# Reordering the head of a fused linear-attention + gated-unit kernel: first halves of two v projections ahead of their second halves, two tiles averaged ahead of either's centring

## Chip, cores, metric

One core of a Trainium2 chip. The metric is device time in microseconds (us) for one execution. "Fast" is the undisturbed state of a run; all comparisons use fast runs. The span is the time from the first to the last instruction of a profiled execution; the granted clock is the share of full speed that TensorE was allowed.

## The reference, cut to what matters

```python
def reference(A_x, A_wqkv, A_w_phi, A_wo, B_x, B_w_gate, B_w_up, B_w_down):
    xn = _layernorm(A_x, axis=-1)                  # 2048 tokens x 512
    # _A_ref: qkv = xn @ wqkv; softmax feature maps of q and k (32 heads of 16); linear attention; @ wo
    # _B_ref: ((xn @ w_gate) * (xn @ w_up)) @ w_down, inner width 1792
    return A_x + _A_ref(xn, ...) + _B_ref(xn, ...)
```

## The kernel before

The 2048 tokens are 16 tiles of 128. Only the first microseconds matter here. Tiles 0 to 3 are centred as soon as x lands (ACT and DVE each average one half of tiles 0 to 2), turned by TensorE (PE), copied by ACT or DVE out of PSUM (the memory that PE writes to), and multiplied by the v weights. Their scaling by the standard deviation is done later.

A v projection of one tile is four 128x512 matmuls into one PSUM bank. The first half of them (h = 0) reads the first half of the v weights and the first half of the tile's turned columns; the second half (h = 1) reads the others. The two halves of the weights are two DMAs.

```python
    load_x(0, 1)                 # on SP
    load_x(1, 1, ACT)
    load_x(2, 2)
    load_v(SP, 1)                # second half of the v weights, 256 KB
    load_gu(SP, 0, (1,))         # first up weights
    act(sbf("lnv", 0, 1), eps_f, ["eps"], ["pace"])
    load_v(ACT, 0)               # first half of the v weights, 256 KB
    load_gu(ACT, 0, (0,))        # first gate weights
    # ... cut: further loads on SP

    def ln_mean_split(t):        # ACT: sum of columns 256.. ; DVE: sum of columns ..256
        act(xn_tile(t)[:, 256:], x_tile(t)[:, 256:], [("x", t)], [("mu", t)], scale=1.0 / 512.0,
            accum=mu[:, t:t + 1])
        dve(lambda e: e.tensor_scalar(out=xn_tile(t)[:, :256], ..., accum_out=mua[:, t:t + 1]),
            [("x", t)], [("mua", t)], 256)

    def ln_center_split(t):      # two DVE instructions of 256 columns
        for h in range(2):
            dve(lambda e, hs=hs: e.tensor_scalar(..., op0=ALU.subtract, op1=ALU.subtract),
                [("x", t), ("mua", t), ("mu", t)], [("xn", t, h)], 256, 0.27)

    def v_matmul(t, b, hs=(0, 1)):
        for h in hs:
            mm(bank(b), [(xnT(q, t * 128, 128), wv_v[:, q, :]) for q in (2 * h, 2 * h + 1)],
               ([("xnT", t, h)] if t < 2 else [("xnT", t)]) + [("wv", h)], b, start=h == 0, stop=h == 1)

    warm(7)
    warm(1, 512, [("x", 0)])
    sc.pin = True                # from here on the order written is the order run, on every engine
    ln_mean_split(0)
    ln_center_split(0)
    ln_mean_split(1)
    ln_center_split(1)
    ln_mean_split(2)
    x_transpose(0, 2, 0, 2)      # tile 0, bank 2, half 0; copied out by ACT
    x_transpose(0, 3, 1, 2)
    warm(1, 256)                 # a matmul on constants, meant to keep PE's clock up
    x_transpose(1, 4, 0, 2, DVE)
    x_transpose(1, 5, 1, 2, DVE)
    warm(1, 256)
    ln_center_whole(2)
    ln_mean(3)
    ln_center(3)
    v_matmul(0, 0)
    v_matmul(1, 1, (0,))
    x_transpose(2, 6)
    v_matmul(1, 1, (1,))
    # ... cut: two up/gate units in halves, v of tiles 2 and 3, then the long main part
```

The softmax here doesn't subtract the row's maximum and nothing guards it: scores larger than these inputs give would overflow.

## Time and profile before

| | before |
|---|---|
| time | 221.97 us, median of 3 (221.96 to 222.13) |
| profiled span | 219.8 us, granted clock 1.0 |
| PE busy | 215.8 us |

From the profile page, part 1 (busy us, share of the span, instructions by engine) and part 4 (the chain of waits, share of the span by engine):

```profile
PE 215.8 (98%) x1276; PEld 105.3 (48%) x1276; DVE 143.0 (65%) x251; ACT 87.6 (40%) x168; POOL 53.7 (24%) x119
...
PE 96%; DMA 2%; SPq 0%; issue 0%; DVE 0%
```

PE and PEld are TensorE's matmuls and weight loads, DVE, ACT and POOL the other engines, SPq the queue that issues DMAs. PE is the bound almost everywhere, so time can only be saved where PE idles. The timeline of PE in the head shows start, length, line and shapes, and in brackets PE's idle time and what ended it (L441 are the transposes, L670 the warm-ups, L224 the projections):

```profile
4.60 0.54 PE L441 MATMUL ps<-arena 128*128 128x128 bf16 x4 [0.20 <-DVE arena L392]
4.98 0.27 PE L670 MATMUL ps<-const-bfloat16-1.0 128*128 128x256 bf16 x1
5.58 0.54 PE L441 MATMUL ps<-arena 128*128 128x128 bf16 x4 [0.32 <-DVE arena L392]
5.96 0.27 PE L670 MATMUL ps<-const-bfloat16-1.0 128*128 128x256 bf16 x1
6.06 0.59 PE L224 MATMUL ps<-arena 128*128 128x512 bf16 x2
7.00 1.02 PE L224 MATMUL ps<-arena 128*128 128x512 bf16 x4 [0.34 <-DMA arena<-in_A_wqkv_dram]
```

There are three gaps. The two matmuls at 6.06 are v of tile 0, first half; the four from 7.00 are its second half and v of tile 1, first half. Which gap costs time is told by the chain that ended last (start, length, what), its first pieces:

```profile
1.70 5.16 DMA arena<-in_A_wqkv_dram
6.86 0.14 issue
7.00 1.02 PE ps L224 x4
8.02 0.22 PE ps L441 x4
```

The chain goes from PE at 7.00 to the DMA of the second v weights, issued at 1.70 and landed at 6.86. It touches neither DVE nor the transposes: shortening the gaps at 4.60 and 5.58 would only lengthen the one at 7.00.

### The profile page before, as it was taken

What the parts mean: (1) busy time and instruction counts of PE and PEld (TensorE: products, weight loads), DVE (VectorE), ACT (ScalarE), POOL (GpSimd) and SP (SyncE); (2) the same over time, 40 slices, a digit from 0 to 9 for tenths busy, and PEclk for the clock granted to TensorE, in tenths of its full rate; (3) what the DMA queues carried; (4) which work ended last, traced back from release to release, by engine and by line L of the source; (5) the groups of instructions that cost most, each with busy time, mean ns of one, the idle gap of its engine ahead of it and who ended that gap; (6) DMA issues with size and microseconds to landing.
All of it is one profiled execution on the core that took longest, in us unless ns stands there. A gap on an engine that the chain in (4) does not pass through costs nothing.

```text
span 219.8 us, 3329 instructions
## 1 busy us (share of the span) xinstructions
PE 215.8 (98%) x1276; PEld 105.3 (48%) x1276; DVE 143.0 (65%) x251; ACT 87.6 (40%) x168; POOL 53.7 (24%) x119
## 2 busy tenths in 40 slices
PE   7999999999999999999999999999999999999995
PEld 2574444444444444544444444544454444454453
DVE  3846899989176654675486565797867777445341
ACT  5558965468753435333445525531122211000000
POOL 3031274323122202220241422224332222200000
PEclk9999999999999999999999999999999999999999
DMA  5998582039910000000002220333764555342221
GB/s 188 277 313 277 146 194 49 0 63 352 185 25 0 0 3 0 0 0 3 0 0 49 48 48 2 73 73 77 162 144 101 116 108 115 84 103 73 64 59 48
DMA packets 47249, 19.91 MB, mean 91 GB/s; under 512 B 37504, under 2 KB 46720, under 8 KB 47232
## 3 DMA queue, kind: packets, MB, share of 16 engines
q1 hardware_dynamic: 46288, 19.03, 36.6%
q10 hardware_dynamic: 944, 0.66, 1.0%
q8 instruction: 10, 0.16, 0.3%
q14 instruction: 7, 0.06, 0.1%
HBM read 8.67 MB, written 2.10 MB: 49 GB/s over the span
## 4 chain that ended last, share of the span: by engine, by line
PE 96%; DMA 2%; SPq 0%; issue 0%; DVE 0%
PE ps L224 91%; DMA arena<-in_A_wqkv_dram 2%; PE ps L569 2%; PE ps L522 2%; PE ps L336 1%; SPq L249 0%; PE ps L441 0%; DVE arena L651 0%
## 5 line engine op out<-in xcount | busy, mean ns | idle before, releaser
L224 PE MATMUL ps<-arena 128*128 128x512 bf16 (+3 forms) x962 | 207.2, 371 | 0.3 <-DMA arena<-in_A_wqkv_dram 0.3
L224 PEld LDWEIGHTS ps<-arena 128*128 128x128 bf16 x962 | 90.9, 98 | 98.4 <-ACT arena L205 0.8
L205 ACT ACTIVATE arena<-ps 128x512 bf16<-128x512 f32 (+3 forms) x116 | 64.4, 594 | 87.6 <-PE ps L224 74.5
L472 DVE TENSOR_REDUCE arena<-arena 128x64 f32<-128x1024 bf16 x32 | 38.5, 1213 | 21.6 <-ACT arena L205 21.6
L627 DVE TENSOR_TENSOR arena<-ps,arena 128x512 bf16<-128x512 f32 x56 | 38.3, 686 | 20.9 <-PE ps L224 17.1
L482 POOL TENSOR_TENSOR arena<-arena 128x512 bf16<-128x512 bf16 x32 | 33.8, 1056 | 1.2
L480 POOL TENSOR_TENSOR arena<-arena 128x32 f32<-128x32 f32 x32 | 8.5, 266 | 96.4 <-DVE arena L476 51.0
L651 DVE TENSOR_TENSOR arena<-ps,arena 128x512 bf16<-128x512 f32 (+2 forms) x13 | 8.5, 651 | 21.5 <-PE ps L224 21.5
L205 ACT ACTIVATE arena<-arena 128x512 bf16<-128x512 bf16 (+4 forms) x31 | 14.6, 495 | 4.1 <-DMA arena<-in_A_x_dram 1.9
L205 ACT ACTIVATE arena<-ps,arena 128x512 bf16<-128x512 f32 x16 | 10.0, 686 | 5.7 <-PE ps L224 5.7
L590 DVE TENSOR_TENSOR arena<-ps,arena 128x512 bf16<-128x512 f32 x16 | 11.1, 692 | 0.6
L363 DVE BATCH_NORM_STATS2 arena<-arena 128x6 f32<-128x512 bf16 x16 | 10.4, 667 | 0.0
L510 DVE TENSOR_TENSOR arena<-ps,arena 128x512 bf16<-128x512 f32 x14 | 9.0, 641 | 0.0
L476 DVE RECIPROCAL arena<-arena 128x64 f32<-128x64 f32 x16 | 8.5, 534 | 0.0
L522 PEld LDWEIGHTS ps<-arena 128*128 128x128 bf16 x128 | 6.2, 97 | 3.8
L569 PEld LDWEIGHTS ps<-arena 128*128 128x128 bf16 x128 | 6.2, 97 | 3.8
L569 PE MATMUL ps<-arena 128*128 128x68 bf16 x128 | 6.7, 194 | 0.0
L522 PE MATMUL ps<-arena 128*128 128x68 bf16 x128 | 6.7, 194 | 0.0
L589 DVE RECIPROCAL arena<-arena 128x32 f32<-128x32 f32 x16 | 5.6, 353 | 0.6
L421 POOL TENSOR_SCALAR arena<-arena 128x1 f32<-128x1 f32 x12 | 2.9, 265 | 12.2 <-ACT arena L205 12.2
L478 DVE RECIPROCAL arena<-arena 128x32 f32<-128x32 f32 x16 | 5.4, 345 | 0.2
L580 POOL TENSOR_SCALAR arena<-arena 128x32 f32<-128x32 f32 x4 | 1.2, 291 | 16.3 <-DVE arena L472 16.3
(35 smaller groups left out, 43.8 us busy)
## 6 DMA issues: line engine op xcount, KB each, us to landing
out_dram<-arena SPq DMA_DIRECT2D x15, 128.0 KB, 1.7
arena<-in_B_w_down_dram SPq DMA_DIRECT2D x1, 1792.0 KB, 8.0
arena<-in_A_x_dram SPq DMA_DIRECT2D x3, 512.0 KB, 3.8
arena<-arena SPq DMA_TRANSPOSE x44, 3.1
arena<-in_B_w_gate_dram SPq DMA_DIRECT2D x1, 640.0 KB, 8.7
arena<-in_B_w_up_dram SPq DMA_DIRECT2D x1, 640.0 KB, 9.7
arena<-in_B_w_gate_dram SPq DMA_DIRECT2D x1, 512.0 KB, 5.0
arena<-in_B_w_up_dram SPq DMA_DIRECT2D x1, 512.0 KB, 6.0
```

Source lines behind the costliest of these rows:

```text
L205: return sc.step(ACT, lambda e: e.activation(out=out_ap, in_=in_ap, func=func, scale=scale, **kw), reads, writes, 130.0 + 0.833 * n)
L224: ins = e.matmul(out_ap, lhsT=l, rhs=r, start=start and i == 0, stop=stop and i == npair - 1, **kw)
L363: dve(lambda e: e.bn_stats(stats_v[:, t, 0:6], x_tile(t)), [("x", t)], [("st", t)], 512)
L472: dve(lambda e: e.tensor_reduce(out=sm, in_=e_v, axis=AX.X, op=ALU.add), [(name, s, 0), (name, s, 1)], [("sums", sr)], 1024)
L476: dve(lambda e: e.reciprocal(out=rs, in_=sm), [("sums", sr)], [("rs", s)], 64, 6.5)
L480: pool(lambda e: e.tensor_tensor(out=rat, in0=sm[:, :, 0], in1=rs[:, :, 1], op=ALU.mult), [("sums", sr), ("rs", s)], [("rat", s)], 32)
L482: pool(lambda e: e.tensor_tensor(out=e_v[:, :, 1, :], in0=e_v[:, :, 1, :], in1=rat[:, :, None].to_broadcast([128, H, 16]), op=ALU.mult), [ ...
L510: dve(lambda e: e.tensor_tensor(out=vs_tile(t)[:, :, 0:16], in0=src.rearrange("p (h f) -> p h f", h=H), in1=rp.unsqueeze(2).to_broadcast([ ...
L522: ins = e.matmul(bank(c // 4, (c % 4) * CW, CW), lhsT=ek[:, c * 128:(c + 1) * 128], rhs=vs[:, c * CW:(c + 1) * CW], start=(t == 0 and c % ...
L569: ins = e.matmul(bank(b0 + c // 4, (c % 4) * CW, CW), lhsT=ph[:, c, :], rhs=kvz_v[:, c, :], start=True, stop=True)
L590: dve(lambda e: e.tensor_tensor(out=o_tile(t).rearrange("p (b h f) -> p b h f", b=2, f=16), in0=nd[:, :, :, 0:16], in1=w_v[:, r].unsqueeze ...
L627: dve(lambda e: e.tensor_tensor(out=hT_v[:, ft, sg * 512:(sg + 1) * 512], in0=bank(bu), in1=g, op=ALU.mult), [("ps", bu), ("g", s)], [("hT ...
```

## The change

The intent is to have v of tile 1, first half, run in the gap before the second weights land, and to have its data there in time. Both tiles are averaged before either is centred, the average of tile 2 (which waits for a later piece of x) goes behind the copies out of PSUM, and the two warm-ups are halved.

```diff
     ln_mean_split(0)
+    ln_mean_split(1)
     ln_center_split(0)
-    ln_mean_split(1)
     ln_center_split(1)
-    ln_mean_split(2)
     x_transpose(0, 2, 0, 2)
     x_transpose(0, 3, 1, 2)
-    warm(1, 256)
+    warm(1, 128)
     x_transpose(1, 4, 0, 2, DVE)
     x_transpose(1, 5, 1, 2, DVE)
-    warm(1, 256)
+    warm(1, 128)
+    ln_mean_split(2)
     ln_center_whole(2)
     ln_mean(3)
     ln_center(3)
-    v_matmul(0, 0)
+    v_matmul(0, 0, (0,))
     v_matmul(1, 1, (0,))
+    v_matmul(0, 0, (1,))
     x_transpose(2, 6)
     v_matmul(1, 1, (1,))
```

## The prediction

> **What bounds the kernel now.** TensorE: busy 215.8 of the 219.8 us span (page, part 1); the chain of waits is 96% PE. From 7.00 us to the last matmul, PE's start-to-start spacings (timeline) never exceed one matmul, so only the head can win. PE idles there 0.2 us before the transposes of tile 0 (start 4.60), 0.32 before those of tile 1 (5.58), and 0.34 before the second half of tile 0's v projection (7.00, released by the weights' DMA). The chain runs back from 7.00 to that DMA (issued 1.70, all parts landed 6.86), not to DVE or ACT: the two earlier gaps are off it.
>
> **What the change does.** No work goes except two warm-up matmuls cut from 256 to 128 columns.
> - Now: v0 first half (two 128x512 matmuls, from 6.06), wait, at 7.00 v0 second half, v1 first half, transposes of tile 2, v1 second half. Matmuls start 0.2155 us apart, as the Trainium skill's "TensorE: Matmul & The Clock Gate", "Back-to-back issue gap", gives (N/2.4 + 2.5 ns: 216 ns at 512).
> - After: v1's first half needs only the first half of the weights (landed 5.63) and tile 1's first transposed half, so it runs in the gap. After the landing PE has two matmuls less: 2 x 0.2155 = 0.43 us.
>
> **Does the head deliver?** My estimate from the trace's durations and pitches: averaging both tiles first puts tile 0's centring 0.1 later (4.20 to 4.30), its transposes at 4.70; tile 1's centring comes 0.35 earlier (5.17 to 4.82), transposes at 5.22. Tile 2's average no longer stands before the evictions on ACT (it waited for x until 5.08), so they start near 5.1 instead of 5.49. v0 first half then waits for its weights: about 5.77. Tile 1's copies on DVE end near 5.9 and 6.15, so v1's first half runs about 6.20 to 6.63. v0's second half stays at about 7.00, idle before it 0.34 to 0.4. Tile 2 is centred by 6.9, before its transposes at 7.43.
>
> **Is it kept?** What follows moves up by 0.43 and must find its data: gate weights landed 7.72 (needed 8.08), up weights 8.52 (needed 9.6), evictions of tiles 2 and 3 follow PE, the key fold has over 2 us of slack. After that PE is the bound, so the gain should survive.
>
> **Predicted time: 221.55 us** (221.97 - 0.43), 80% range 221.3 to 221.95. Chances: faster by over 2% 0.01, within 2% 0.98, slower by over 2% 0.01.
>
> **What would show each step right or wrong.**
> - v0 second half still starts at about 7.0, released by the weights' DMA.
> - v1 first half lies wholly before it; tile 2's transposes start at about 7.43 (before: 7.86), the first up projection at 8.08 (before: 8.51).
> - PE's span is shorter by 0.43 from there on, with no new idle.
> - Tile 0's transposes start about 0.1 later, tile 1's about 0.35 earlier.
>
> **What would make it wrong.**
> - The landing moves from run to run; with an early one in unprofiled runs the old order lost less: gain 0.3 or below.
> - Tile 2's centring or the gate weights come late: gain 0.1 to 0.3.
> - The clock, granted full from 4.72 us on: less warm-up work could lose it. The same page, "The HAM clock gate", gives windows of about 3.4 us and half rate; one would cost up to 1.7 us (estimate). Unlikely: idle stays under 0.4 us at a time.
> - Unpinned DVE/ACT work is reordered by the kernel's own scheduler; PE's slack should hide that.

## The result, and the profile after

| | before | after |
|---|---|---|
| time, median of 6 | 221.91 us (221.41 to 222.13) | 221.51 us (220.91 to 221.63) |
| ratio, 95% interval | | 0.998 (0.9965 to 0.9995) |
| profiled span | 219.8 us | 219.7 us |

Ratios here and below are the mean time of one kernel's fast runs over the mean of the other's of the same rounds, so they are not quite the ratios of the medians.

The medians differ by 0.40 us, the means by 0.44. The profiled spans differ by only 0.1 us, and the trace tells why. PE's timeline in the changed kernel:

```profile
4.69 0.65 PE L441 MATMUL ps<-arena 128*128 128x128 bf16 x4 [0.30 <-DVE arena L392]
5.14 0.31 PE L670 MATMUL ps<-const-bfloat16-1.0 128*128 128x128 bf16 x1
5.24 0.63 PE L441 MATMUL ps<-arena 128*128 128x128 bf16 x4
5.67 0.31 PE L670 MATMUL ps<-const-bfloat16-1.0 128*128 128x128 bf16 x1
5.79 1.33 PE L224 MATMUL ps<-arena 128*128 128x512 bf16 x4
7.31 0.59 PE L224 MATMUL ps<-arena 128*128 128x512 bf16 x2 [0.18 <-DMA arena<-in_A_wqkv_dram]
```

Four 128x512 matmuls now stand before the wait and two behind it, instead of two and four. The wait ends at 7.31 instead of 7.00, because in this execution the weights landed later. The chain:

```profile
1.71 5.46 DMA arena<-in_A_wqkv_dram
7.17 0.14 issue
7.31 0.59 PE ps L224 x2
7.90 0.22 PE ps L441 x4
```

So the profiled execution lost 0.31 us to a later landing and won the rest back. This can be freed of the luck of the landing: take the span minus the start of v0's second half (both from the instruction records, which have more digits than the page). Before: 219.85 - 7.00 = 212.85 us. After: 219.72 - 7.31 = 212.42 us, rounded from 212.415. The difference is 0.43 us, which is two matmuls at the spacing of 0.2155 us.

One caution on the page after: its trace holds 1252 matmul records where the trace before holds 1276, so its PE busy time (214.8 us) and a few small gaps in its chain come from missing records, not from idle time.

### The profile page after: what moved, and what is told of

The parts are those of the page before. It is cut to its first block, busy times and chain, and to the rows that moved or that the text cites. A ratio compares the mean times of both kernels' runs of the same rounds, so it can differ in the third digit from the quotient of the medians.

```text
span 219.7 us, 3305 instructions
## 1 busy us (share of the span) xinstructions
PE 214.8 (98%) x1252; PEld 105.6 (48%) x1276; DVE 143.2 (65%) x251; ACT 87.8 (40%) x168; POOL 53.9 (25%) x119
## 4 chain that ended last, share of the span: by engine, by line
PE 95%; DMA 2%; issue 1%; SPq 0%; DVE 0%
PE ps L224 90%; DMA arena<-in_A_wqkv_dram 2%; PE ps L569 2%; PE ps L522 2%; PE ps L336 1%; SPq L249 0%; PE ps L441 0%; DVE arena L651 0%
## 5 line engine op out<-in xcount | busy, mean ns | idle before, releaser
L224 PE MATMUL ps<-arena 128*128 128x512 bf16 (+3 forms) x938 | 205.2, 372 | 1.5 <-DMA arena<-in_A_wqkv_dram 0.2
L224 PEld LDWEIGHTS ps<-arena 128*128 128x128 bf16 x962 | 91.0, 98 | 98.4 <-ACT arena L205 0.7
```

Of the source, the lines that this page charges most:

```text
L224: ins = e.matmul(out_ap, lhsT=l, rhs=r, start=start and i == 0, stop=stop and i == npair - 1, **kw)
```

## The experiments

Twelve runs were made, in three calls of four (E1 to E4; the changed kernel again, E5, E9, E10; E9 again, E11, E12, E8). Each call has its own runs of the kernel before. The three calls ran on three different chips, so times are best compared within a call. Names: v0 and v1 are the v projections of tiles 0 and 1. Theory A is the prediction's: two matmuls pass from behind the landing to ahead of it. Theory B says the gain comes from the new averages and the earlier tile 1. Theory C says both parts are needed.

This table has all the traces but those of E3 and E4, in which the clock fell (us; "landing" is the last of the 16 parts of the second v weights).

| run | order of halves | landing | start of v0's second half | span | span minus start |
|---|---|---|---|---|---|
| before | old | 6.86 | 7.00 | 219.85 | 212.85 |
| E2 head only | old | 7.35 | 7.49 | 220.34 | 212.85 |
| E10 | old | 6.45 | 6.59 | 219.45 | 212.86 |
| E12 | old | 6.25 | 6.39 | 219.24 | 212.85 |
| after | new | 7.17 | 7.31 | 219.72 | 212.42 |
| changed kernel again | new | 7.24 | 7.38 | 219.80 | 212.42 |
| E1 order only | new | 7.41 | 7.55 | 219.95 | 212.40 |
| E9 | new | 6.31 | 6.55 | 218.97 | 212.42 |
| E9 again | new | 6.47 | 6.73 | 219.15 | 212.42 |
| E11 | new | 6.42 | 6.88 | 219.30 | 212.42 |
| E8 no warm-ups | new | 6.86 | 6.99 | 219.57 | 212.58 |
| E5 tile 2 ahead too | new | 7.12 | 7.17 | 219.56 | 212.39 |

### E1: the new order of the halves alone

Kernel before with:

```diff
-    v_matmul(0, 0)
+    v_matmul(0, 0, (0,))
     v_matmul(1, 1, (0,))
+    v_matmul(0, 0, (1,))
```

> The kernel before with the new order of the v projection's halves alone; averages, centring and warm-ups as before. Theory A (two matmuls, 0.43 us, pass from behind the landing of the second weights to ahead of it): full gain, 0.35 to 0.43 us against before; in its trace v1's first half starts near 6.5, v0's second half 0.13 after the landing. Rival B (the gain is tile 1's earlier centring and transposes): gain under 0.15 us. Rival C (both are needed, as the matmuls come too late without the new head): 0.1 to 0.3 us, and v0's second half starts later than landing + 0.14.

Measured: 221.47 us (before 221.76), ratio 0.9987, interval 0.9969 to 1.0005. The mean gain is 0.29 us, which misses theory A's 0.35 to 0.43 and lies in theory C's range; the interval reaches zero, so the time alone would not settle it. The trace does. PE's timeline of E1:

```profile
6.13 1.03 PE L224 MATMUL ps<-arena 128*128 128x512 bf16 x4
7.55 0.59 PE L224 MATMUL ps<-arena 128*128 128x512 bf16 x2 [0.39 <-DMA arena<-in_A_wqkv_dram]
```

Four matmuls ahead of the wait, and after it the 212.40 us of the changed kernel, with the old head. v1's first half was started at 6.56, as expected. Theory B fails on the trace, and at this landing (7.41) C does too: v0's second half started 0.14 us behind it. With the old head PE is through with v1's first half at 6.99 in this trace, so C could only hold for landings before about 6.86 (estimate). That the mean gain is 0.14 us short of 0.43 would follow if E1's runs had later landings than those of the kernel before; landings of unprofiled runs are not on record.

### E2: the new head alone

Changed kernel with the three `v_matmul` lines put back:

```diff
-    v_matmul(0, 0, (0,))
+    v_matmul(0, 0)
     v_matmul(1, 1, (0,))
-    v_matmul(0, 0, (1,))
```

> The changed kernel with the old order of the v halves: new averages, centring and short warm-ups alone. Theory A: no gain (within 0.15 us of before): v0's first half starts near 5.8 instead of 6.06, but its second half still 0.13 us after the landing, and PE waits there 0.25 us longer than before. Rival B: gain of 0.3 us or more.

Measured: 222.12 us, ratio 1.0025, interval 0.9996 to 1.0053. No gain, as theory A has it, though the expected 0.15 us either way was missed on the slow side. PE's timeline of E2:

```profile
5.98 0.59 PE L224 MATMUL ps<-arena 128*128 128x512 bf16 x2 [0.23 <-DMA arena<-in_A_wqkv_dram]
7.49 1.02 PE L224 MATMUL ps<-arena 128*128 128x512 bf16 x4 [0.92 <-DMA arena<-in_A_wqkv_dram]
```

The better head only waits longer (0.92 us), and what follows the wait is the 212.85 us of the old order. The expectation that v0's first half starts near 5.8 was missed (5.98), because its own weights landed at 5.84. One of the six timed runs took 223.81 us at a granted clock of 0.992; the other five average 222.05, still 0.25 us over the mean of before (221.80). Whether this rest is a chance of the landings was not settled.

### E3 and E4: the second weights later, with the new and with the old order

In the changed kernel (E3) and in the kernel before (E4):

```diff
-    load_v(SP, 1)
     load_gu(SP, 0, (1,))
+    load_v(SP, 1)
```

> The changed kernel with the second half of the v weights issued after the first up weights, so that it lands later (about 8.5 instead of 6.9 to 7.2). Theory A: the time moves with the landing, about 1.3 to 1.7 us slower than the changed kernel, and is 0.43 us under the next run of this call (same delay, old order). A theory that the landing does not bound expects no loss.

> The kernel before with the same delay of the weights. Theory A: 1.3 to 1.7 us slower than before, as v0's second half starts 0.13 us after the later landing, and 0.43 us slower than the run with the new order and the same delay. Rival B (earlier tile 1 is what counts): as slow as that one.

Measured: E3 223.66 us (222.39 to 224.98), ratio 1.0077, interval 1.0035 to 1.0118. E4 224.43 us (223.35 to 233.96), ratio 1.0116, interval 1.0081 to 1.0150. The delay costs time, as theory A has it, but the sizes cannot be read, because something else came in. Three of six E3 runs, and two of the five fast E4 runs, had a granted clock of 0.992 (E4's sixth run, 233.96 us, was slow; its execution is the one profiled). E3's three runs at full clock average 222.60 us; its three at 0.992 average 224.72. E4's three fast runs at 0.999 or 1.0 average 223.73 us (223.35 to 223.96), 1.13 us over E3's three at full clock. The sign agrees, but the distance is over twice the expected 0.43 us, and with so few runs, and no fast trace of E4, it stays unexplained.

The trace of E3 shows the clock. First PE's timeline, then busy times by stretch (PE, PEld, DVE, ACT, POOL, granted clock, DMA share, GB/s):

```profile
5.77 1.02 PE L224 MATMUL ps<-arena 128*128 128x512 bf16 x4
8.62 0.90 PE L224 MATMUL ps<-arena 128*128 128x512 bf16 x2 [1.83 <-DMA arena<-in_A_wqkv_dram]
```

```profile
5.40:8.70 3.30, 1.36 (x9) 0.52 (x8) 3.06 (x11) 1.23 (x5) 0.00 (x0) 1.00 1.07 338
8.80:12.10 3.30, 3.30 (x17) 2.07 (x16) 1.39 (x4) 0.60 (x1) 0.78 (x3) 0.50 1.25 232
12.20:15.60 3.40, 3.35 (x24) 2.35 (x24) 0.00 (x0) 2.10 (x5) 1.10 (x4) 1.00 0.90 313
```

In the first stretch PE was busy 1.36 of 3.30 us, and in the next the clock was half. Its record falls to 0.5 at 8.77 us and comes back at 12.18. The Trainium skill's "TensorE: Matmul & The Clock Gate", section "The HAM clock gate", describes such windows of 3413 ns, and the record's 3.413 us agrees to the digit. In this trace the span minus the start of v0's second half is 214.10 us, 1.68 more than in the traces at full clock: half of 3.41 us. A wait for weights can thus be followed by a cost of its own. That the long wait brings it about rests on counts: 5 of the 11 fast runs with late weights had the clock of 0.992, one of E2's six, and one of the 33 runs of the kernel before.

### The changed kernel again

> The changed kernel once more, as the yardstick of this call and for a second trace. Theory A: 0.2 to 0.6 us under before; whatever its landing is, the span minus the start of v0's second half is 212.41 us (0.01 to 0.03 either way), as in the two earlier traces with the new order, against 212.85 in the two with the old.

Measured: 221.37 us (before 221.75), ratio 0.997, interval 0.9934 to 1.0006. One of the eleven runs of before took 224.01 us at a clock of 0.992; without it, the means are 221.75 and 221.28, a gain of 0.46 us. The trace gives 212.42 us after the start of v0's second half, as expected.

### E5: the transposes of tile 2 into the gap too

```diff
-    v_matmul(0, 0, (1,))
     x_transpose(2, 6)
+    v_matmul(0, 0, (1,))
     v_matmul(1, 1, (1,))
```

> The changed kernel with the transposes of tile 2 (four of 128 columns, 0.22 us) ahead of v0's second half too. Theory A: span minus the start of v0's second half falls by another 0.22 us, to 212.19; but tile 2 is centred at about 6.99 us, so its transposes start at about 7.05 and end at 7.27: with a landing after 7.13 the gain is up to 0.22 us, with one at 6.9 it is nothing. On average 0 to 0.2 us under the changed kernel. A rival by which the number of matmuls after the landing does not matter expects none at any landing.

Measured: 221.35 us, ratio 0.9973, interval 0.9942 to 1.0005; as fast as the changed kernel of the same call (means 221.32 and 221.28). The transposes did run in the gap, earlier than expected:

```profile
6.73 0.40 PE L441 MATMUL ps<-arena 128*128 128x128 bf16 x4
7.17 1.64 PE L224 MATMUL ps<-arena 128*128 128x512 bf16 x8
```

The first line is the four transposes of tile 2. The eight matmuls of the second line (the piece names only the first one's shape) are four of v and the four half-width ones of the first gate projection; they take 1.64 us to the end of the last. In the records the first gate matmul starts 0.38 us after the last v matmul instead of 0.22, so PE stood still for 0.16 us; the gate weights had landed 0.05 us before it started (8.16 and 8.21). The 0.22 us won was mostly lost to the next transfer in line: span minus start came to 212.39, not the expected 212.19.

### E9 and E10: the first gate weights out of the way

Changed kernel (E9) and kernel before (E10) with:

```diff
-    load_gu(SP, 0, (1,))
+    load_gu(SP, 0)
     act(sbf("lnv", 0, 1), eps_f, ["eps"], ["pace"])
     load_v(ACT, 0)
-    load_gu(ACT, 0, (0,))
```

The gate weights are needed after all the v weights, but on ACT's queue they flowed at the same time. The Trainium skill's "DMA: Bandwidth & Descriptors", "Issuing engines are not separate DMA queues", says that transfers of all issuing engines run on the same 16 DMA engines and interleave; now the SP queue has them in the order of need.

> The changed kernel with the first gate weights taken from ACT's queue and issued on SP behind the second v weights, so that these need not share the DMA engines with them. If the landing bounds: it comes near 6.2 instead of 6.9 to 7.2, v0's second half starts at about 6.65, right behind v1's first half, and the first up projection at about 7.75 instead of 7.96 to 8.08: 0.3 to 0.6 us under the changed kernel. If the gate weights then land after 7.6, part of it is lost; if the transfers are bound by something other than sharing, the landing stays and so does the time.

> The kernel before with the same earlier landing of the second v weights. Theory A: with the wait gone, the order of the halves is worth nothing any more: v0's second half starts at about 6.50 behind its first half, the first up projection at about 8.0; 0.5 to 0.8 us under before, and only 0.2 to 0.3 us behind the run of the changed kernel with the same loads (that rest is the earlier start of v0's first half, 5.79 against 6.06). If the change were worth its 0.43 us whatever the landing, that distance would be 0.43 us.

Measured: E9 220.84 us, ratio 0.9954, interval 0.9922 to 0.9985. E10 221.22 us, ratio 0.9971, interval 0.9940 to 1.0003. The second v weights landed at 6.31 and 6.45 instead of 6.86 to 7.41, as the page would have it. Sharing may not be all: in E9 the gate weights, issued 0.44 us later than in the trace after, landed earlier too (7.20 and 8.25), and the bytes moved in the first 8 us hardly differ between the traces (1.76 to 1.85 MB with the old loads, 1.82 to 1.88 with the new). Why was not settled. PE's timeline of E9 has no wait any more:

```profile
5.69 1.46 PE L224 MATMUL ps<-arena 128*128 128x512 bf16 x6
6.98 0.39 PE L441 MATMUL ps<-arena 128*128 128x128 bf16 x4
7.21 1.03 PE L224 MATMUL ps<-arena 128*128 128x512 bf16 x6
```

The first six are v0's first half, v1's first half and v0's second half, back to back. Its chain of waits has moved away from those weights and, as the view has it, into the head:

```profile
0.79 2.60 DMA arena<-in_A_x_dram
...
3.41 0.57 DVE arena L385 x3
...
4.18 0.27 DVE arena L392
...
4.50 0.54 PE ps L441 x4
5.04 0.06 PE ps L670
5.09 0.46 PE ps L441 x4
5.55 0.06 PE ps L670
5.61 0.08 issue
5.69 1.46 PE ps L224 x6
```

The view puts x, the averages (L385), the centring (L392) and even the warm-ups (L670) on the chain. But the 0.08 us called "issue" before 5.69 hide a wait for the other half of the v weights. From the DMA view of E9 (KB, us from issue to landing; issued at 1.28 on ACT and 1.71 on SP):

```profile
arena<-in_A_wqkv_dram ACTq DMA_DIRECT2D x1, 256.0 KB, 4.3
arena<-in_A_wqkv_dram SPq DMA_DIRECT2D x1, 256.0 KB, 4.6
```

In the records the first half landed at 5.555 and v0's first half started at 5.690, 0.135 us later, though its columns had been copied by 5.20. This distance is 0.135 or 0.136 us in all nine traces with the new head, and 0.235 to 0.432 us in the five with the old one. So the new head is good enough to wait for the first v weights, and in E9 their landing, with six matmuls back to back behind it, is the bound. E9 is 0.40 us under the changed kernel of its call (means 220.88 and 221.28), and the fastest kernel.

For E10 the expectation was partly wrong. It said that the wait would be gone, so that the distance to E9 would be 0.2 to 0.3 us. But E10's weights landed at 6.45, still later than its first half was done, and v0's second half still started 0.135 us behind the landing. Its means are 0.39 us behind E9 (221.27 and 220.88). The wait had become shorter, not gone.

### E9 again, E11 and E12: which part counts once the weights come early

E11 is E1 with the loads of E9; E12 is E2 with the loads of E9.

> The changed kernel with the first gate weights behind the v weights, once more, as yardstick: 0.7 to 1.1 us under before. v0's second half right behind v1's first half (near 6.55), span minus its start 212.41 us.

> New order of the halves with the old averages and centring, gate weights behind. With the weights landing near 6.3 to 6.45, PE gets to v0's second half late by itself: v0's first half starts at 5.94 to 6.06 (old head), v1's first half 0.43 later, v0's second half at 6.8 to 6.9, no wait for the DMA. So 0.25 to 0.35 us slower than the yardstick: at an early landing the new head, worth nothing before, is worth that much.

> New averages and centring with the old order of the halves, gate weights behind. v0's first half near 5.7, its second half at the landing + 0.135, so 6.45 to 6.6; span minus that start 212.85. Against the yardstick 0.3 to 0.45 us slower, about like the old head and old order with the same loads (221.22 in the call before), for which the landing binds too.

| with the loads of E9 | old order of halves | new order |
|---|---|---|
| old head | E10 221.27 | E11 221.10 |
| new head | E12 221.13 | E9 again 220.86 |

These are mean times; E10 was in the call before, on another chip, in which E9 gave 220.88. Medians and ratios to the kernel before: E9 again 220.85, 0.9945 (0.9923 to 0.9968); E11 221.02, 0.9956 (0.9933 to 0.9980); E12 221.16, 0.9959 (0.9935 to 0.9983). The new order alone is now worth 0.17 us, and both parts together about 0.4. The 0.14 us between E10 and E12 is no gain of the head: in both traces v0's second half starts 0.135 us behind the landing, with 212.85 or 212.86 us to follow, and E12's weights landed 0.20 us earlier (6.25 and 6.45). The head pays only on top of the new order (E11 to E9 again), and the order pays less without the head; so at an early landing theory C holds in part. E11 is 0.24 us behind E9 (0.25 to 0.35 was expected), E12 0.27 us (0.3 to 0.45 was expected). The first lines of L224 in E11 and of the wait in E12 show the two reasons:

```profile
6.02 1.46 PE L224 MATMUL ps<-arena 128*128 128x512 bf16 x6
```

```profile
5.63 0.59 PE L224 MATMUL ps<-arena 128*128 128x512 bf16 x2
6.39 1.02 PE L224 MATMUL ps<-arena 128*128 128x512 bf16 x4 [0.17 <-DMA arena<-in_A_wqkv_dram]
```

E11 starts its six matmuls late (6.02, 0.33 us behind the first landing) and has no wait; E12 starts early (5.63, 0.135 us behind it) and then waits. In the trace of E9 again v0's second half started at 6.73, not near 6.55, as the first v weights landed at 5.73 instead of 5.555; the 212.42 us after it came as expected.

### E8: no short warm-ups

Changed kernel without both `warm(1, 128)` lines.

> The changed kernel without the two short warm-up matmuls of 128 columns. They stand in idle time of PE, so if the clock does not fall back the time is that of the changed kernel (within 0.15 us; 0.2 to 0.6 us under before), and granted clock 1.0 in all runs. If they keep the clock up, some runs show a clock of 0.992 and 1.5 to 2 us more, as the runs did in which PE waited 1 to 2 us for the weights.

Measured: 221.51 us (221.16 to 223.12), ratio 0.9984, interval 0.9953 to 1.0015. The granted clock was 0.999 or 1.0 in all six runs, so taking them out did not make the clock fall here; six runs cannot exclude a rare fall. The one run of 223.12 us had a clock of 1.0 and is not explained; so had one of 223.46 us of the kernel before.

The trace holds a second lesson. The weights landed early (6.86), v1's second half was done early, and the six matmuls from there on took

```profile
7.64 1.19 PE L224 MATMUL ps<-arena 128*128 128x512 bf16 x6
```

instead of the 1.03 us of the six at 7.21 in E9. The first gate projection waited 0.15 us, and its weights had landed at 8.18, 0.05 us before its start. This is why E8's line in the table reads 212.58.

## Why the prediction was right

The predicted time was 221.55 us, the measured one 221.51; the predicted gain was 0.43 us, the measured difference of the medians 0.40, of the means 0.44.

- **The bound in the head is the landing of the second v weights.** Right. In the traces with a wait there, v0's second half starts 0.13 to 0.14 us behind the landing, wherever that is between 6.25 and 7.41 (E5, which has the transposes in between, is the exception with 0.05).
- **Two matmuls, 0.43 us, leave the part behind the landing.** Right, and the best-shown point: span minus start is 212.85 or 212.86 us in four traces with the old order, and 212.40 to 212.42 in six with the new, with either head and either order of loads.
- **The head's gaps are off the chain.** Right for the loads as they were: the head alone (E2) gave no gain. Once the second weights land early, a slow head does cost time if the order is the new one (E11 against E9 again).
- **v0's first half waits for its weights, about 5.77.** Right: 5.79, 0.135 us behind their landing.
- **v0's second half at about 7.00.** The cause was right, the time was not: 7.31 in that execution; tile 2's transposes (7.74) and the first gate projection (8.39, in the prediction "the first up projection") were as late against 7.43 and 8.08. A single trace had been read as if the landing were fixed, and its landing was an early one: that execution took 221.57 us, 0.40 less than the median of the timed runs. By the constant rest a landing near 7.26 goes with the median (estimate). The predicted gain does not depend on it as long as v1's first half is done before the landing.
- **v1's first half from 6.20 to 6.63.** It ran from 6.53 in the trace after, because full clock was granted only at 6.42 us, not at 4.72 as in the trace before; with full clock at 5.73 (the changed kernel again) it ran from 6.21. Its delay was hidden in the wait, with some luck: PE was through with it at 6.96, and with the landing of the trace before (6.86, start at 7.00) only 0.04 us would have been left.
- **Tile 0's transposes 0.1 us later, tile 1's 0.35 earlier.** 0.09 later and 0.33 earlier.
- **The data that follow are there in time.** Right in the two traces of the changed kernel, but with less room than the prediction gave. It took the gate weights to land at 7.72, 0.36 us before they were needed. In the trace after they landed at 8.25 and the gate projection started at 8.39; in E5 and E8 they cost 0.15 to 0.16 us.
- **The clock as a risk.** It did not strike the changed kernel in 12 runs. That it is real is shown by E3.

What stays open: the distance between E3 and E4, why the landing of one transfer moves by up to 0.55 us between executions whose loads are the same, and whether the shorter wait makes the fall of the clock rarer than in the kernel before (one of the 33 runs of before had a clock of 0.992, none of 12 of the changed kernel: too few to tell).

## What to carry to other kernels

When the chain of waits runs to a landing, the gain of a reordering is the work that passes from behind that landing to ahead of it, and time saved upstream of the landing only lengthens the wait. Compare two traces from the moment of the landing on, not from the start: a constant remainder shows an effect of 0.4 us that timings with a scatter of the same size hardly do. Then look at the order of the transfers themselves: putting a later-needed load behind the needed one gave 0.40 us more, and made the new head matter, which alone had gained nothing, on top of the new order. And check a chain of waits against the landings themselves: the one of E9 runs through warm-ups, while the start of v0's first half keeps the same distance from the landing of its weights in nine traces.

## What the Trainium skill lacked or had wrong

- "TensorE: Matmul & The Clock Gate", "Why this matters for your kernels", asks for no PE idle gaps of over about 3 us. In E3 (one trace) a single gap of 1.83 us in a window in which PE was busy 1.36 of 3.30 us was followed by 3.41 us at half clock, and the three runs with a clock of 0.992 took 2.1 us more than the three at full clock. In E2's trace a gap of 0.92 us passed without a fall.
- The same page, "What's actually happening" (the two states of the clock) and "Seeing it yourself" (a third, 13/16): the slow profiled execution of E4, on one core, shows a granted clock of 0.949 for its last 218 us, which is none of the three; its 128x512 matmuls mostly started 0.224 us apart there instead of 0.216. No cause is known.
- The same page, "Back-to-back issue gap": N/2.4 + 2.5 ns agrees, with 0.2155 us measured between starts of 128x512 matmuls. The figure of about 131 ns for such matmuls in a stream, on the same page, does not: in no trace here did two of them start less than 0.214 us apart.
- "DMA: Bandwidth & Descriptors" gives no scatter from execution to execution for a landing. The same 256 KB transfer, in the same order of loads, landed between 6.86 and 7.41 us after the span's start in seven traces (before, E1, E2, E5, E8, and twice the changed kernel).
